# Out projection inside the second attention, and attention layers in a hand-made issue order, on one Trainium2 core

## The chip, the cores and the metric

The kernel runs on one core of one Trainium2 chip (trn2). The metric is device time in microseconds (us) of one execution. Each kernel was timed in turn with the kernel before, on the same chip and in the same rounds. The experiments came in five batches on five chips, so kernels of different batches are compared by their ratios to the kernel before (whose medians lay between 1346.9 and 1352.4 us) and by the stages of their profiles.

Engine names in the profile: PE is TensorE (PEld its weight loads), DVE is VectorE, ACT is ScalarE, POOL is GpSimd, SP is SyncE. A name with q (SPq) is the sequencer of that engine that issues DMA transfers. L408 is line 408 of the kernel that the line belongs to. PSUM is the memory that matmuls write to; an eviction is the op that copies a result out of it.

## The reference

Four layers in the order A B A B, each added to its input, on x of 2048 rows by 576 columns. Cut to what matters:

```python
def _A_ref(x, wqkv, wo):            # sliding-window attention, 32 heads of 18
    qkv = (x @ wqkv)                # -> q, k, v
    # every query looks at 8 keys: its own row and rows 2, 4, ..., 14 before it
    logits = einsum('bhsd,bhswd->bhsw', q, kg) * scale
    o = einsum('bhsw,bhswd->bhsd', softmax(masked logits), vg)
    return o.reshape(B, S, D) @ wo

def _B_ref(x, w_in, w_sp, b_sp, w_out):      # gated MLP with a mix over rows
    z = gelu(x @ w_in)                       # 576 -> 4608
    z1, z2 = halves of z                     # 2304 each
    z2 = layernorm(z2)
    g = w_sp @ z2 + b_sp[:, None]            # 2048 x 2048 over rows
    return (z1 * g) @ w_out                  # 2304 -> 576

x = x + A(layernorm(x)); x = x + B(layernorm(x))
x = x + A(layernorm(x)); x = x + B(layernorm(x))
```

## The kernel before

**Attention.** The rows are cut into 19 query tiles of 112 rows, each with 16 rows of halo, and the 32 heads into two halves. That makes 38 steps. A step computes logits (16 small matmuls, `L_mm`), exponentials on ScalarE (`EXP`), a mask on VectorE (`MASK`), the product with V (`PV`) and the division by the row sum (`NORM`). The result of a tile is transposed by a DMA (`TAIL_A`) and goes through the output projection `wo` and the residual add (`TAIL_B`). Then it is normalised for the next layer and transposed again. The projections to Q, K and V are spread over the steps. The program order below is only a proposal: a scheduler fixes the order on each engine, and it is told to put the next logits ahead.

```python
        def pr(off):
            return tc.high_priority(offset=off) if off > 0 else nullcontext()
        for s in range(NSTEP):                     # cfg.prio = 200, cfg.prio2 = 0
            with pr(cfg.prio2):
                EXP(s)
                MASK(s)
            if s + 1 < NSTEP:
                with pr(cfg.prio):
                    L_mm(s + 1)
            if s >= 1:
                with pr(cfg.prio2):
                    PV(s - 1)
                    NORM(s - 1)
            for fn in table.get(s, []):            # Q/K, V, tail work of this step
                fn()
        # ... [cut] where the tail of tile t goes (plast = its second step):
            for (off, fn) in ((2, TAIL_A(t)), (4, TAIL_B(t)), (5, TAIL_B2(t)), (6, TAIL_C(t))):
        # steps after the Q/K work also get two junk matmuls each (JUNK)
```

Every third eviction of Q/K is on VectorE, the others on ScalarE, and the moves that lay the heads out (`QK<-stg`) go over three engines' queues:

```python
                use_dve = (self.evac_rr % 3 == 0)
                if use_dve:
                    nc.vector.tensor_copy(out=dst, in_=pp[:, :])
                else:
                    nc.scalar.copy(out=dst, in_=pp[:, :])
                # ... [cut] one move of 72 KB per head: sync, gpsimd or scalar queue in turn
```

**B layer.** First the "norm stage": 16 tiles of z2, gelu, statistics and normalisation. Each tile is normalised by nine ops of 256 columns, most of them on VectorE, the rest on GpSimd. Then the "mixer": z1, the 2048 by 2048 mix, bias and product. Then a separate out projection, whose weights are loaded only when the mixer's buffers are free:

```python
        def p1_norm(i):
            for b in range(NB):                    # NB = 9 blocks of 256 columns
                if b >= NB - NPOOL_NORM:
                    nc.gpsimd.tensor_scalar(out=z2b[b][:, i, :], ...)
                else:
                    nc.vector.tensor_scalar(out=z2b[b][:, i, :], ...)
        # ... [cut] mixer
        wout_b = p3.tile([P, NJ - NJA, D], bf16, name="wout_b", bufs=1)
        for j in range(NJA, NJ):
            self.dma(wout_b[:, j - NJA, :], wv_[:, j, :], eng=(nc.sync, nc.gpsimd)[j % 2])
        # ... [cut] then 16 row tiles: p3_mm (36 matmuls), residual add, statistics, normalise, transpose
```

The softmax here doesn't subtract the row's maximum and nothing guards it: scores larger than these inputs give would overflow.

## Time and profile before

The kernel before takes 1347.1 us (median of four runs, 1344.7 to 1348.4). The page of the profile gives TensorE as the busy engine. These are whole lines of its parts 1 (busy time), 2 (busy tenths in 40 slices of the span; PEclk is the granted TensorE clock in tenths of full speed) and 4 (the chain of work that ended last):

```profile
span 1348.4 us, 21451 instructions
...
PE 1249.9 (93%) x8656; PEld 659.5 (49%) x8656; DVE 616.5 (46%) x1402; ACT 384.2 (28%) x595; POOL 356.4 (26%) x487
...
PE   1999969989999999998998987899999999999997
...
PEclk9999989999999999997999999899999999999999
...
PE 62%; DVE 11%; POOL 10%; issue 7%; DMA 6%; ACT 3%; SPq 1%; ACTq 0%; POOLq 0%; DVEq 0%
...
```

TensorE is busy 93% of the time, and the clock is near full almost everywhere. A gain can come only from the 7% of gaps and from matmuls that could be left out. The view of stretches cuts the span at the stages. Its columns are the stretch, its length, busy time and instruction count of each engine (PE, PEld, DVE, ACT, POOL), the granted clock, the DMA share and GB/s:

```profile
...
46.50:188.00 141.50, 125.74 (x1771) 78.17 (x1771) 102.60 (x240) 82.76 (x111) 70.90 (x59) 0.96 0.63 114
...
274.30:605.00 330.70, 326.96 (x1515) 147.58 (x1512) 104.11 (x161) 39.35 (x44) 9.82 (x20) 1.00 0.05 16
605.00:690.00 85.00, 77.18 (x582) 58.56 (x581) 36.06 (x99) 13.01 (x15) 17.05 (x39) 0.92 0.71 200
690.00:849.00 159.00, 141.19 (x1840) 84.94 (x1839) 107.49 (x248) 88.92 (x120) 77.30 (x96) 0.97 0.62 125
...
```

From the top: the steps of the first attention (TensorE busy 126 of 141.5 us), the first mixer (327 of 331, fixed by the matmuls), the first out projection (77 of 85), and the second attention (141 of 159). The last out projection, not shown, takes 84 us, TensorE busy in 73. The view of TensorE's waits from 605 to 849 us (who waited for whom, us in total, times, longest) shows how little is lost:

```profile
...
PE po_6066 L941 <- DMA wout_b<-in_B_w_out_dram: 7.1, 6, 2.1
PE O_ps L540 <- DVE ln_rstd L163: 4.0, 9, 0.7
PE pw L582 <- DMA oT_7004<-o_t_6991: 3.9, 1, 3.9
...
```

The wait for w_out at the start of the projection is the largest.

VectorE closes the loop of the norm stage. This is its timeline (start, duration, operation, and in brackets the idle time before it):

```profile
...
229.40 0.34 DVE L848 TENSOR_SCALAR z2b_3093<-zp,z_mean,z_rstd 128x256 bf16<-128x256 bf16 x1 [0.67 <-POOL z_rstd L835]
...
231.10 1.77 DVE L819 CUSTOM_DVE_ANT_0 z_junkD<-zp 128x1536 bf16<-128x1536 bf16 x1
...
234.41 0.35 DVE L848 TENSOR_SCALAR z2b_3093<-zp,z_mean,z_rstd 128x256 bf16<-128x256 bf16 x1 [0.67 <-POOL z_rstd L835]
...
```

From 229.40 to 234.41 is one period of 5.02 us (start times are rounded). Six such ops of 256 columns, then a sum of squares of 1.77 us and small ops.

### The profile page before, as it was taken

The numbers are of one execution on the slowest core, as the hardware profiler recorded it, in microseconds if no ns is written. First come the engines' busy times: TensorE is split into PE (matmuls) and PEld (weight loads), VectorE is DVE, ScalarE is ACT, GpSimd is POOL, SyncE is SP. The second block draws the span as 40 slices with busy tenths as digits, with TensorE's granted clock in tenths as the row PEclk, the third lists the DMA queues.
The fourth block names the chain that finished last, engine by engine and source line by source line (L and its number), as shares of the span: only waits on it lengthen the run. The fifth ranks groups of instructions, "written<-read, shape, count | busy, mean of one in ns | idle before, by whom it ended". The sixth has DMA issues, their size and how long they took to land.

```text
span 1348.4 us, 21451 instructions
## 1 busy us (share of the span) xinstructions
PE 1249.9 (93%) x8656; PEld 659.5 (49%) x8656; DVE 616.5 (46%) x1402; ACT 384.2 (28%) x595; POOL 356.4 (26%) x487
## 2 busy tenths in 40 slices
PE   1999969989999999998998987899999999999997
PEld 0456644434444444445754655444444444444576
DVE  4468858843322332332534878588323223333221
ACT  2556726620011111001126665465101111100000
POOL 7445547830000000002141646488000000000111
PEclk9999989999999999997999999899999999999999
DMA  9449759020000000009653677861100000000232
GB/s 264 98 94 145 121 134 214 1 90 6 9 10 9 10 9 9 0 4 266 179 137 62 151 145 129 181 125 41 43 9 9 10 9 9 2 7 1 72 113 67
DMA packets 180128, 101.04 MB, mean 75 GB/s; under 512 B 138276, under 2 KB 162212, under 8 KB 180028
## 3 DMA queue, kind: packets, MB, share of 16 engines
q1 hardware_dynamic: 170208, 84.15, 28.1%
q10 hardware_dynamic: 6364, 8.55, 2.2%
q0 software_dynamic: 3456, 6.96, 2.2%
q8 instruction: 68, 1.11, 0.3%
q14 instruction: 32, 0.26, 0.1%
HBM read 41.16 MB, written 16.52 MB: 43 GB/s over the span
## 4 chain that ended last, share of the span: by engine, by line
PE 62%; DVE 11%; POOL 10%; issue 7%; DMA 6%; ACT 3%; SPq 1%; ACTq 0%; POOLq 0%; DVEq 0%
PE pg L904 36%; PE po L941 9%; DVE z_junkD L819 4%; PE pp L412 3%; DMA QK<-stg 2%; POOL ln_xn_84 L181 2%; POOL ln_xn_81 L181 1%; POOL ln_rstd L164 1%; POOL z_rstd L835 1%; POOL ln_xn_83 L181 1%; POOL ln_xn_82 L181 1%; DMA wout_b<-in_B_w_out_dram 1%; DMA wv_sb<-in_A_wqkv_dram 1%; DMA win2b<-in_B_w_in_dram 1%; DVE z_msq L828 1%
## 5 line engine op out<-in xcount | busy, mean ns | idle before, releaser
L908 DVE TENSOR_TENSOR g_tmp<-pg,bsp 128x512 f32<-128x512 f32 x144 | 99.4, 692 | 435.5 <-PE pg L904 423.9
L412 PE MATMUL pp<-xnT,wqk_sb 128*128 128x512 bf16 x400 | 100.7, 394 | 29.8 <-DMA xnT<-ln_xn_84 28.5
L812 PEld LDWEIGHTS <-xnT 128*128 128x128 bf16 x800 | 78.4, 98 | 97.0 <-issue 13.0
L812 PE MATMUL pz<-win2a,xnT 128*128 128x512 bf16 x384 | 103.1, 379 | 5.9 <-ACT zp L816 4.4
L164 POOL TENSOR_TENSOR ln_rstd<-ln_rstd,neg_half 112x1 f32<-112x1 f32 (+2 forms) x70 | 43.4, 621 | 152.3 <-DVE ln_rstd L163 152.1
L812 PE MATMUL pz<-win2b,xnT 128*128 128x512 bf16 x256 | 77.0, 386 | 6.9 <-DMA win2b<-in_B_w_in_dram 6.9
L816 ACT ACTIVATE zp<-pz 128x1024 bf16<-128x1024 f32 x64 | 65.0, 1020 | 44.6 <-POOL z2b_9746 L845 18.9
L412 PEld LDWEIGHTS <-wqk_sb 128*128 128x128 bf16 x400 | 36.9, 100 | 71.2 <-issue 36.0
L819 DVE CUSTOM_DVE_ANT_0 z_junkD<-zp 128x1536 bf16<-128x1536 bf16 x32 | 56.9, 1777 | 18.7 <-ACT zp L816 18.7
L370 PE MATMUL pv<-wv_sb,xnT 128*128 128x288 bf16 (+1 forms) x380 | 62.2, 286 | 0.2 <-DVE stg L418 0.2
L76 POOL DMA_DIRECT2D wout_b<-in_B_w_out_dram x14 | 7.5, 541 | 172.4 <-PE pg L904 172.4
L76 POOL DMA_DIRECT2D QK<-stg x52 | 31.5, 608 | 73.0 <-ACT stg L420 28.0
L584 DVE TENSOR_TENSOR x_new<-pw,xo 112x288 f32<-112x288 f32 (+1 forms) x76 | 33.5, 445 | 18.0 <-PE pw L582 10.7
L420 ACT CAST stg<-pp 128x512 bf16<-128x512 f32 x54 | 31.0, 585 | 37.4 <-PE pp L412 22.7
L370 PEld LDWEIGHTS <-xnT 128*128 128x128 bf16 (+1 forms) x380 | 33.5, 97 | 15.8 <-issue 1.4
L489 PE MATMUL L_ps<-QK 18*128 18x112 bf16 (+1 forms) x1216 | 32.0, 210 | 4.9 <-DMA QK<-stg 1.7
L418 DVE CAST stg<-pp 128x512 bf16<-128x512 f32 x26 | 18.0, 691 | 37.0 <-PE pp L412 33.5
L159 DVE BATCH_NORM_STATS2 ln_st<-x_new 112x6 f32<-112x288 f32 (+1 forms) x76 | 33.9, 449 | 1.2
L489 PEld LDWEIGHTS <-QK 18*128 18x128 bf16 (+1 forms) x1216 | 20.4, 93 | 25.6 <-issue 21.6
L845 POOL TENSOR_SCALAR z2b_3101<-zp,z_rstd,z_nmr 128x256 bf16<-128x256 bf16 x16 | 32.4, 2024 | 0.0
L845 POOL TENSOR_SCALAR z2b_9746<-zp,z_rstd,z_nmr 128x256 bf16<-128x256 bf16 x16 | 32.4, 2023 | 0.0
L904 PE MATMUL pg<-W_sb,z2b_3093 128*128 128x512 bf16 x128 | 28.4, 379 | 1.9 <-DVE z2b_3093 L848 1.9
(549 smaller groups left out, 2513.3 us busy)
## 6 DMA issues: line engine op xcount, KB each, us to landing
xres_73<-x_new SPq DMA_DIRECT2D x18, 252.0 KB
xo<-xres_74 SPq DMA_DIRECT2D x18, 252.0 KB
xres_75<-x_new SPq DMA_DIRECT2D x18, 252.0 KB
QK<-stg POOLq DMA_DIRECT2D x52, 72.0 KB, 3.8
win2a<-in_B_w_in_dram SPq DMA_DIRECT2D x2, 1728.0 KB
QK<-stg SPq DMA_DIRECT2D x48, 72.0 KB
wqk_sb<-in_A_wqkv_dram ACTq DMA_DIRECT2D x4, 576.0 KB
out_dram<-ob SPq DMA_DIRECT2D x16, 144.0 KB
```

What stands on the lines that cost most here:

```text
L164: nc.gpsimd.tensor_tensor(out=rstd[:nrows, :], in0=rstd[:nrows, :], in1=self.neg_half[:nrows, :], op=ALU.pow)
L181: e.tensor_scalar(out=xn[:nrows, 0:D], in0=x_t[:nrows, :], scalar1=mv[:nrows, 0:1], scalar2=rstd[:nrows, 0:1], op0=ALU.subtract, op1=ALU.mult)
L370: nc.tensor.matmul(pv[:nk, 0:288], lhsT=self.xnT[:, c, QT * t:QT * t + nk], rhs=wv_sb[:, c, hh * 288:(hh + 1) * 288], start=(c == 0), stop ...
L412: nc.tensor.matmul(pp[:, :], lhsT=wqk_sb[:, c, wc0:wc0 + P], rhs=self.xnT[:, c, col0:col0 + 512], start=(c == 0), stop=(c == 4))
L489: nc.tensor.matmul(L_ps[:nk, j, ftl * QT:ftl * QT + nq], lhsT=kT[32 * j:32 * j + DH, g, QT * t:QT * t + nk], rhs=qT[32 * j:32 * j + DH, g, ...
L812: nc.tensor.matmul(pzvs[ci][:, sub * 512:sub * 512 + w], lhsT=self.xnT[:, c, PADL + i * P:PADL + (i + 1) * P], rhs=win2(c)[:, c0 + sub * 5 ...
L816: nc.scalar.activation(out=zp[:, c0:c0 + cn], in_=pzvs[ci][:, 0:cn], func=ACT.Gelu_apprx_tanh, accum_out=sums[:, ci:ci + 1])
L819: nc.vector.tensor_tensor_reduce(out=junkD[:], in0=zp[:, 0:SQ_D], in1=zp[:, 0:SQ_D], scale=1.0, scalar=0.0, op0=ALU.mult, op1=ALU.add, acc ...
L845: nc.gpsimd.tensor_scalar(out=z2b[b][:, i, :], in0=zp[:, b * 256:(b + 1) * 256], scalar1=rstd[:, 0:1], scalar2=nmr[:, 0:1], op0=ALU.mult, ...
L904: nc.tensor.matmul(pg[:, :], lhsT=z2b[jj][:, i, sub * P:(sub + 1) * P], rhs=W_sb[:, i, q * 512:(q + 1) * 512], start=(i == 0), stop=(i == ...
L908: nc.vector.tensor_tensor(out=tmp[:], in0=pg[:, :], in1=bsp[:, q * 512:(q + 1) * 512], op=ALU.add)
L941: nc.tensor.matmul(acc[hh], lhsT=uT[j // 2][:, j % 2, i * P:(i + 1) * P], rhs=wout_j(j)[:, hh * 288:(hh + 1) * 288], start=(j == 0), stop= ...
```

## The change

The intent is to fill the gaps of one stage with the work of another. The out projection of the first B layer is to run inside the second attention, whose steps leave TensorE idle. Therefore its weights are loaded during the mixer, and the mixer's results stay in place in one set of buffers (`zc`). The Q/K projections go in five chunks of rows, so that attention can start before all rows are known. In the attention layers the order on every engine is written by hand (`manual_schedule`), with no scheduler, no priorities and no junk matmuls. The core of the diff, with cuts:

```diff
-        for s in range(NSTEP):
-            with pr(cfg.prio2):
-                EXP(s)
-                MASK(s)
-            if s + 1 < NSTEP:
-                with pr(cfg.prio):
-                    L_mm(s + 1)
-            # ... [cut]
+        self.run_deferred()
+        with tc.manual_schedule():
+            run(pro)
+            L_mm(0)
+            for s in range(NSTEP):
+                EXP(s)
+                if s >= 1:
+                    PV(s - 1)
+                    NORM(s - 1)
+                run(tabA.pop(s, []))        # out projection of a tile, V, transposes of o
+                MASK(s)
+                if s + 1 < NSTEP:
+                    L_mm(s + 1)
+                run(tabB.pop(s, []))        # Q/K projections, units of w_out, statistics
+                run(tabE.pop(s, []))        # normalise + transpose, late loads
+        # the tail of tile t:
+        tl = 3 if first else 2
+        for t in range(NT):
+            p_ = 2 * t + 1
+            put(tabA, p_ + 1, t_load, t)
+            put(tabA, p_ + 1, t_oT, t)              # issue the transpose of o
+            put(tabA, p_ + tl, t_half, t, 0)        # use it
+            put(tabA, p_ + tl + 1, t_half, t, 1)
+            put(tabB, p_ + tl + 1, t_stats, t)
+            put(tabE, p_ + tl + 2, t_ln, t)
+        # Q/K: evictions all on ScalarE, one run of columns per head, q and k together
+                nc.scalar.copy(out=stg[:, qk * w:(qk + 1) * w], in_=pp[:, 0:w])
+                        self.dma(QK[c][32 * rg:32 * rg + DH, g, :], stg[...],
+                                 eng=(nc.gpsimd if j7 % 2 else nc.sync))
+        # the fused out projection: a half unit, 18 matmuls into one PSUM buffer
+        def u_half(i, hh):
+            po = self.PT_tile("po")
+            self.p3_mm(i, hh, po)
+            nc.vector.tensor_tensor(out=x3[...], in0=po[:, 0:288], in1=xo3[...], op=ALU.add)
         # B layer
         def p1_norm(i):
-            for b in range(NB):   # nine ops of 256 columns on VectorE and GpSimd
-                # ... [cut]
+            nc.vector.tensor_scalar(out=zc[i // 4][:, i % 4, 256:256 + Fh], in0=zp[:], ...)  # 2304 columns
+        # w_out: two loads of 1.3 MB on GpSimd's queue, written at jj == 2 of the mixer
+            self.dma(self.wout[:, 0:h, :], src[:, 0:h, :], eng=self.nc.gpsimd)
+        # second half of w_in (2.3 MB): one load on the sync queue at step 14 of the first attention
+            self.dma(win2[:, 0:4, :], self.B_w_in[0:512, Fh:2 * Fh].rearrange("(c p) n -> p c n", p=P))
```

Outside the attention layers the scheduler still decides.

## The prediction

> **What bounds the kernel now.** By the table of stretches: first attention 0 to 188 us; its B layer's norm stage to 274, mixer to 605, out projection to 690; second attention to 849; norm to 935, mixer to 1264.5, out projection to 1348. In the mixers TensorE is 100% busy: the chain of waits shows blocks of 18.13 us for 84 matmuls of 512 columns, 0.216 us each. About 660 us are so fixed. Gaps are elsewhere: attention steps after the Q/K work take 2.85 us with PE busy 61 of 72 us and DVE 60, partly junk matmuls (88, 27 us summed); steps with Q/K take about 5.3 us. The norm stage repeats every 5.02 us, against 4.86 us of matmul issue: by the timeline VectorE closes that loop (six normalise ops 1.70, square-sum 1.70, small ops 0.93, a 0.67 us wait on GpSimd). It opens with a 3.9 us wait for a weight load. Both out projections open with waits for w_out (12 us stretches, PE busy 5.3 and 9.1 us).
>
> **What the change does, by stage.**
> - Mixer: same matmuls, in the same order; results go in place into shifted columns. About 0.
> - Norm: one VectorE op of 2304 columns replaces six of 256 and three on GpSimd. The six follow each other at 0.26 us, too short for one column per cycle plus overhead. The Trainium skill, "VectorE: DVE Perf Modes", section "Side-by-side: where the cycles go for N=2048 bf16", gives about 0.69 us for 2048 columns in the fastest mode; estimate 0.8 us here. The loop falls to about 4.1, so TensorE binds at 4.86; weights are loaded early. 86.3 becomes about 79: -7, twice.
> - Last out projection: weights preloaded. 576 matmuls at 0.1225 us = 70.6 plus a 7 us end, against 84: -6.
> - First out projection plus second attention: now 244 us. Matmul issue in the fused stage, by traced rates: projection 70.6, Q/K 44, V 23.5, out 23.5, logits 12, PV 16 = 190 us, junk gone. Prologue 45, 38 steps averaging 4.0 us of PE work with 5 to 10% of stalls, tail 7: about 226. -18.
> - First attention: nothing fused to fill with. In the new order VectorE's mask of a step precedes PV, then V and out matmuls, then the residual add, then the next mask: 1.1 + 0.5 + 0.6 + 0.7 + 0.55, about 3.5 us a step, slightly more with Q/K. 38 steps make about 137, starting at about 43 instead of 46.5: 185 against 188. -3.
>
> Summed: -41 to -46 us.
>
> **Predicted: 1304 us**, 8 in 10 between 1278 and 1328. Faster by over 2%: 0.82; within 2%: 0.15; slower: 0.03.
>
> **What would show it.** Right: norm period about 4.9 us, the 2304-column op under 1 us; mixer end to second norm stage 215 to 237 us, PE busy above 85%; first attention 175 to 192; no wait for w_out at the end; mixer blocks still 18.1 us. Wrong: the wide normalise near 2.4 us; PE waiting on masks or transposes in fused steps, or on Q/K moves at a chunk's first logits (160 moves a layer instead of 64, 70 on GpSimd at 0.6 us of issue each).
>
> **What would make it wrong.** Fixed order: a late transpose, move or eviction blocks the matmuls behind it, and nothing overtakes. Three shared PSUM buffers serve all projections; all Q/K and V evictions are on ScalarE. The first attention could lose 10 us so. With near perfect overlap the fused stage nears 205 us, and the total 1280.

## The result, and the profile after

The kernel after is correct and takes 1434.6 us (median of four runs, 1430.3 to 1436.6). The ratio is 1.0648, 95% interval 1.0617 to 1.0678: slower. Ratios here are the mean time of one kernel's fast runs over that of the other's in the same rounds, so they are not quite the ratio of the medians quoted.

The same parts of the page:

```profile
span 1434.9 us, 21392 instructions
...
PE 1261.4 (88%) x8592; PEld 676.7 (47%) x8668; DVE 575.8 (40%) x1200; ACT 420.1 (29%) x696; POOL 244.7 (17%) x371
...
PE   5677869989999999998766776689899999999999
...
PEclk9797969999999999999888998679999999999999
...
PE 76%; DMA 9%; ACT 4%; DVE 4%; issue 2%; SPq 1%; POOL 1%; ACTq 0%; DVEq 0%; POOLq 0%
...
```

TensorE has nearly the same number of matmuls as before: 8668 weight loads instead of 8656, that is 100 more Q/K matmuls (narrower ones) and no junk ones (88). (Of the matmuls themselves only 8592 were recorded.) Yet it is busy 11 us longer, and its clock has dips to 0.6, 0.7 and 0.8 in the two attention stages, where before has one 7 and two 8s. In the row PE the dips stand at the same places. The view of stretches of the kernel after, from the top: the steps of the first attention, the first mixer, and the fused stage in three parts, namely the prologue (the work before the first logits), the steps from the first logits to the last, and the tail:

```profile
...
39.70:217.30 177.60, 129.97 (x1748) 82.29 (x1748) 110.31 (x257) 97.62 (x155) 93.04 (x109) 0.82 0.50 118
...
296.60:631.70 335.10, 327.70 (x1483) 148.34 (x1512) 101.64 (x151) 38.95 (x42) 4.29 (x6) 0.99 0.06 18
631.70:675.60 43.90, 38.54 (x280) 27.11 (x278) 12.37 (x35) 12.86 (x22) 13.12 (x38) 1.00 0.60 175
675.60:933.10 257.50, 181.89 (x2091) 121.11 (x2092) 116.03 (x272) 100.97 (x157) 88.70 (x111) 0.86 0.43 109
933.10:945.90 12.80, 6.74 (x69) 3.83 (x66) 6.44 (x20) 1.51 (x3) 3.67 (x4) 0.50 0.43 104
...
```

The steps of the first attention take 177.6 us (before: 141.5). The fused stage takes 43.9 + 257.5 + 12.8 = 314.2 us, of which TensorE is busy 38.5 + 181.9 + 6.7 = 227.2. Its prologue takes what was predicted (45); the loss is in the steps. Before, projection and attention together took 85 + 159 = 244. The norm stage and the last projection became shorter (table below), and the mixer became longer.

This table takes the stages from the first and last matmuls of the traces, in us. Later columns belong to experiments told below:

| stage | before | predicted | after | x_comb3 | x_auto3 | h1 |
|---|---|---|---|---|---|---|
| first attention with its start | 188.1 | 185 | 217.3 | 193.8 | 195.2 | 198.2 |
| norm stage, first | 86.3 | 79 | 79.3 | 82.2 | 79.2 | 81.9 |
| mixer, first | 330.5 | 330.5 | 335.1 | 328.4 | 327.8 | 328.4 |
| out projection + second attention | 243.7 | 226 | 314.2 | 252.6 | 244.7 | 233.3 |
| norm stage, second | 86.9 | 80 | 78.5 | 79.6 | 78.9 | 82.5 |
| mixer, second | 328.8 | 328.8 | 335.2 | 328.5 | 329.9 | 327.6 |
| last out projection | 84.1 | 78 | 75.3 | 75.2 | 75.2 | 75.2 |
| profiled span | 1348.4 | | 1434.9 | 1340.3 | 1330.9 | 1327.1 |

Against the prediction the fused stage lost 88 us, the first attention 32 and the two mixers 11 together; the rest was right or slightly better.

**What TensorE waits for.** In the fused stage:

```profile
...
PE pw L408 <- DMA oT_5984<-o_t_5981: 21.4, 5, 8.0
PE pw L408 <- DMA oT_5983<-o_t_5980: 18.8, 6, 7.9
PE pw L408 <- DMA oT_5985<-o_t_5982: 14.3, 5, 5.0
PE L_ps L351 <- ACT P_sb_5978 L359: 8.9, 10, 1.9
...
```

The first three lines are one tile with three buffers: 54.5 us in 16 waits for a transposed attention output, up to 8.0 us each. In the first attention it is the same wait, and as large a one for the exponentials that free the logits' PSUM:

```profile
...
PE pw L408 <- DMA oT_113<-o_t_110: 11.2, 3, 6.6
PE L_ps L351 <- ACT P_sb_107 L359: 10.6, 9, 3.8
PE L_ps L351 <- ACT P_sb_108 L359: 10.2, 11, 1.8
...
```

**The longest of these waits, step by step.** TensorE's timeline, at 125 us:

```profile
...
122.13 0.78 PE L329 MATMUL pv<-wv_sb,xnT 128*128 128x288 bf16 x5
...
125.62 0.55 PE L377 MATMUL O_ps<-v_ext_103,P_sb_108 128*128 128x19 bf16 x16
132.78 1.38 PE L408 MATMUL pw<-wo_sb,oT_113 128*128 128x288 bf16 x5 [6.61 <-DMA oT_113<-o_t_110]
133.96 1.40 PE L329 MATMUL pv<-wv_sb,xnT 128*128 128x288 bf16 x5
135.29 0.58 PE L351 MATMUL L_ps<-zc_70 18*128 18x112 bf16 x16
...
```

The five `pw` matmuls wait 6.61 us. Everything that follows in the order waits with them: V, and the logits of the next step; neither shows a wait of its own when its turn comes. Then the clock is low. Five `pv` matmuls take 1.40 us instead of 0.78, and 16 logits 0.58 instead of 0.40. This is what the Trainium skill describes in "TensorE: Matmul & The Clock Gate", section "Part 1: The HAM clock gate (the "warmup" mystery)": an idle window of about 3.4 us lets the clock fall to half, and about 3.4 us of work bring it back. The trace agrees for this wait (1.40 / 0.78 = 1.8; the view of stretches gives a granted clock of 0.50 from 128.3 to 138.5 us). But a wait need not be that long: the clock also went to 0.50 at 107.8, 152.2 and 199.9 us, where no wait just before was longer than 2.2 us and TensorE had been busy for 1.9, 1.7 and 2.2 of the 3.4 us before. Nor does every wait have this effect: of the 16 in the fused stage, 11 were followed by half clock. So a wait is often paid twice. In the two attention stages together TensorE was busy 379.0 us here and 358.0 in x_comb3 (below) for the same matmuls, at a higher clock there and still not a full one. The sync queue in the same microseconds:

```profile
...
117.79 1.20 SPq L64 DMA_DIRECT2D win_119<-in_B_w_in_dram  x2
...
120.64 3.05 SPq L64 DMA_DIRECT2D zc_68<-stg  x4
123.73 0.46 SPq L64 DMA_DIRECT2D xo<-in_A_x_dram  x1
129.54 1.24 SPq L401 DMA_TRANSPOSE oT_113<-o_t_110  x1
...
```

A load of w_in (2.3 MB) is issued at 117.79. Behind it stand a store, four Q/K moves and a small load, and only then, at 129.54, the transpose that TensorE waits for; it takes over 3 us to land. The queue itself stood still for 5.3 us before it, and the profile puts that down to the landing of the load:

```profile
...
SPq L401 <- DMA win_119<-in_B_w_in_dram: 5.3, 1, 5.3
...
```

**Why a step with Q/K work takes 4.5 to 5.5 us.** ScalarE's timeline in the first attention:

```profile
...
92.70 1.71 ACT L359 ACTIVATE P_sb_108<-L_ps 128x896 bf16<-128x896 f32 x2
94.30 0.41 ACT L333 CAST v_ext_102<-pv 128x288 bf16<-128x288 f32 x1
95.99 0.55 ACT L311 CAST stg<-pp 128x464 bf16<-128x464 f32 x1 [1.28 <-PE pp L309]
96.97 0.55 ACT L311 CAST stg<-pp 128x464 bf16<-128x464 f32 x1 [0.43 <-PE pp L309]
97.42 0.87 ACT L145 ACTIVATE ln_xn_73<-x_in_334,ln_nmr,ln_rstd 128x576 bf16<-128x576 bf16 x1
98.19 1.71 ACT L359 ACTIVATE P_sb_107<-L_ps 128x896 bf16<-128x896 f32 x2
...
```

and TensorE's logits in that time:

```profile
...
94.47 0.40 PE L351 MATMUL L_ps<-zc_69 18*128 18x112 bf16 x16 [1.38 <-ACT P_sb_108 L359]
94.81 2.13 PE L309 MATMUL pp<-xnT,wqk_sb 128*128 128x464 bf16 x10
...
```

The logits of the next step are done at 94.87. Their exponentials start at 98.19, 3.3 us later: in ScalarE's order stand a V eviction, two Q/K evictions and a normalise op, and the evictions wait for ten `pp` matmuls. The Trainium skill, "Perfetto Trace Analysis", section "Tensor Engine Instruction (MATMUL, LD_WEIGHTS)", says that ScalarE, VectorE and GpSimd are strict first-in-first-out; this timeline agrees. Late steps without Q/K work do run at about 3.4 us: exponentials start at 170.92, 174.69, 177.93 and 181.12 us.

**The mixer's extra 5 us** is one wait, at its first matmul:

```profile
...
PE pz_4025 L679 <- DMA w_0_4019<-in_B_w_in_dram: 5.8, 1, 5.8
```

This line is from the kernel after. In GpSimd's timeline the two halves of w_out (1.3 MB each) are issued at 297.07 and 300.64 us, ahead of the mixer's own first weights (301.73 on the sync queue), and the bias follows. The scheduler had moved the load there from its place in the text, two blocks later. In the second mixer the same.

### The profile page after: what moved, and what is told of

Read it like the earlier page. It is cut to its first block, busy times and chain, and to the rows that moved or that the text cites. A ratio compares the mean times of both kernels' runs of the same rounds, so it can differ in the third digit from the quotient of the medians.

```text
span 1434.9 us, 21392 instructions
## 1 busy us (share of the span) xinstructions
PE 1261.4 (88%) x8592; PEld 676.7 (47%) x8668; DVE 575.8 (40%) x1200; ACT 420.1 (29%) x696; POOL 244.7 (17%) x371
## 4 chain that ended last, share of the span: by engine, by line
PE 76%; DMA 9%; ACT 4%; DVE 4%; issue 2%; SPq 1%; POOL 1%; ACTq 0%; DVEq 0%; POOLq 0%
PE pg L690 34%; PE pz L616 10%; PE po L212 9%; PE pp L309 5%; PE pw L408 3%; PE pv L329 2%; DMA oT_5983<-o_t_5980 1%; PE L_ps L351 1%; PE pzs L616 1%; ACT P_sb_108 L359 1%; DMA oT_5984<-o_t_5981 1%; DMA oT_5985<-o_t_5982 1%; DMA win_119<-in_B_w_in_dram 1%; PE O_ps L377 1%; ACT stg L311 1%
## 5 line engine op out<-in xcount | busy, mean ns | idle before, releaser
L690 PE MATMUL pg<-W_sb,zc_68 128*128 128x512 bf16 x570 | 148.1, 381 | 0.1
L690 PE MATMUL pg<-W_sb,zc_70 128*128 128x512 bf16 x560 | 146.3, 379 | 1.3
L690 PE MATMUL pg<-W_sb,zc_69 128*128 128x512 bf16 x560 | 146.3, 380 | 0.6
L690 PE MATMUL pg<-W_sb,zc_71 128*128 128x512 bf16 x564 | 146.2, 379 | 0.6
L132 POOL TENSOR_TENSOR ln_rstd<-ln_rstd,neg_half 112x1 f32<-112x1 f32 (+2 forms) x70 | 39.0, 558 | 523.0 <-DMA wo_sb<-in_A_wo_dram 340.6
L309 PE MATMUL pp<-xnT,wqk_sb 128*128 128x464 bf16 (+1 forms) x500 | 112.4, 381 | 11.7 <-DMA xnT<-ln_xn_73 4.1
L616 PEld LDWEIGHTS <-xnT 128*128 128x128 bf16 x800 | 78.9, 99 | 80.9 <-issue 4.8
L690 PEld LDWEIGHTS <-zc_68 128*128 128x128 bf16 x576 | 56.6, 98 | 68.2 <-issue 1.1
L690 PEld LDWEIGHTS <-zc_71 128*128 128x128 bf16 x576 | 56.4, 98 | 68.5 <-DVE zc_71 L643 0.8
L690 PEld LDWEIGHTS <-zc_69 128*128 128x128 bf16 x576 | 56.5, 98 | 68.3 <-issue 0.6
L690 PEld LDWEIGHTS <-zc_70 128*128 128x128 bf16 x576 | 56.4, 98 | 67.7
L329 PE MATMUL pv<-wv_sb,xnT 128*128 128x288 bf16 (+1 forms) x380 | 69.4, 325 | 17.5 <-POOL mask_base L97 13.5
L311 ACT CAST stg<-pp 128x464 bf16<-128x464 f32 (+1 forms) x100 | 50.8, 514 | 101.5 <-PE pp L309 82.9
L309 PEld LDWEIGHTS <-wqk_sb 128*128 128x128 bf16 x500 | 49.7, 106 | 60.8 <-issue 22.5
L619 ACT ACTIVATE zp<-pz 128x1024 bf16<-128x1024 f32 x64 | 65.5, 1024 | 38.7 <-PE pz L616 38.5
L616 PE MATMUL pz<-win_119,xnT 128*128 128x512 bf16 x312 | 72.6, 384 | 1.1 <-DVE x_new L410 0.5
L616 PE MATMUL pz<-win_8983,xnT 128*128 128x512 bf16 x312 | 71.9, 381 | 1.1 <-DVE x_new L410 0.5
L329 PEld LDWEIGHTS <-xnT 128*128 128x128 bf16 (+1 forms) x380 | 41.1, 110 | 33.6 <-POOL mask_base L97 13.5
L386 DVE RECIPROCAL rec<-O_ps 112x16 f32<-112x16 f32 (+1 forms) x76 | 19.2, 253 | 71.9 <-PE O_ps L377 71.7
## 6 DMA issues: line engine op xcount, KB each, us to landing
zc_68<-stg SPq DMA_DIRECT2D x72, 32.6 KB
```

The source lines that it names most:

```text
L132: nc.gpsimd.tensor_tensor(out=rstd[:nrows, :], in0=rstd[:nrows, :], in1=self.neg_half[:nrows, :], op=ALU.pow)
L309: nc.tensor.matmul(pp[:, 0:w], lhsT=Aw["wqk"][:, k_, wc0:wc0 + P], rhs=self.xnT[:, k_, lo:lo + w], start=(k_ == 0), stop=(k_ == 4))
L311: nc.scalar.copy(out=stg[:, qk * w:(qk + 1) * w], in_=pp[:, 0:w])
L329: nc.tensor.matmul(pv[:nk, 0:288], lhsT=self.xnT[:, c, QT * t:QT * t + nk], rhs=Aw["wv"][:, c, hh * 288:(hh + 1) * 288], start=(c == 0), s ...
L616: nc.tensor.matmul(pz[:, k_ * 512:k_ * 512 + w], lhsT=lhs[c], rhs=win2[:, c, c0:c0 + w], start=(c == 0), stop=(c == 4))
L619: nc.scalar.activation(out=zp[:, us[0][0]:us[0][0] + w], in_=pz[:, 0:w], func=ACT.Gelu_apprx_tanh, accum_out=sums[:, ns:ns + 1])
```

## The experiments

The theory to begin with was that the order written by hand is at fault, since a late input blocks everything behind it on its engine (called the order below). Rivals:

- the lead: transposes are issued one step (second attention) or two (first) ahead of their use, too few;
- ScalarE's order: evictions stand ahead of exponentials;
- the fusion: the projection's matmuls delay the attention chain;
- the queue: the sync queue is too full of Q/K moves for transposes to be issued in time. Where an expectation names a theory Q, it is this one.

Eighteen kernels ran on the chip. Unless told otherwise each was timed twice, and h1 and the three of the last batch four times. All gave correct results.

### x_auto: the scheduler's order back

```diff
-        with tc.manual_schedule():
+        if True:
```

> The changed kernel with only the fixed issue order lifted: the scheduler orders all engines again, all else as in the change. Theory A (the fixed order costs the time; fusion and one-run moves are harmless): both attention stages shrink, the first from 217 to about 190 us, the fused one from 313 to about 250, total 1330 to 1350. Rival F (fusing the projection and moving Q/K in 160 moves a layer cost the time themselves): stays above 1410.

1388.4 us (ratio 1.0291, interval 1.017 to 1.041, wide because each side has only two runs: one of the three of the kernel before was an outlier of 4472 us and was left out). Theory A had expected 1330 to 1350. The order is worth 46 us of the loss. But 41 us of loss stay, the first attention still takes 213.6 us, and the fused stage 267.7. The order is a cause and not the only one.

### x_tl4, x_actlate, x_unfused: one rival each, in the fixed order

x_tl4 gives the transposes three steps of lead, the use coming four steps after the tile's last step (and it moved the load of the residual with the use):

```diff
-        tl = 3 if first else 2
+        tl = 4
-            put(tabA, p_ + 1, t_load, t)
+            put(tabA, p_ + tl - 1, t_load, t)
```

> Fixed order kept; the output matmuls of a tile come 4 steps after its last PV instead of 3 and 2 (the residual load moves with them). Theory T (matmuls are stuck behind transposes that the DMA queue delivers late: 54.5 us of such waits in the fused stage and 16 in the first attention[...]): these waits nearly vanish and the total falls by 60 to 90 us, to 1345 to 1375. Rival S (ScalarE's order, evictions and normalise ops standing between one exp and the next, sets the step): the waits move to the exp loop and the gain is 30 us or less.

1434.1 us, where theory T had expected 1345 to 1375. The fused stage fell to 287.0 us, but the first attention rose to 238.7. VectorE now waited for the residual there:

```profile
...
DVE x_new L410 <- DMA xo<-in_A_x_dram: 42.9, 12, 9.4
...
```

That was a flaw of the edit: the residual's load now stood late in the sync queue. It is mended in x_tl4b below.

x_actlate holds the Q/K evictions and the normalise ops of a step back behind the next exponentials on ScalarE (with the transposes and late loads that stand with the normalise ops in `tabE`):

```diff
             for s in range(NSTEP):
                 EXP(s)
+                run([(fn, ()) for fn in late])      # evictions of the step before
+                late.clear()
+                run(tabE.pop(s - 1, []))            # normalise ops of the step before
```

> Fixed order kept; on ScalarE the Q/K evictions and the normalise ops of a step come after the next step's exp instead of before it. Rival S: steps of the first attention with Q/K fall from 5.5 us to about 4.4, so that stage goes from 217 to about 195 us, and the fused one loses 10 to 25 us: total about 1390. Theory T: less than 15 us in all, since the transposes stay late.

1436.2 us: nothing. The waits tell why. In the first attention:

```profile
...
PE pw L422 <- DMA oT<-o_t: 31.1, 10, 8.8
...
PE L_ps L365 <- ACT P_sb L373: 5.2, 2, 5.1
...
```

The wait of the logits for the exponentials fell from 20.8 us (10.6 + 10.2 above) to 5.2, as meant. The wait for the transposes rose from 16.3 us (11.2 + 3.4 + 1.7) to 31.1. One limit went, and the next took all its time.

x_unfused does all 16 units of the out projection ahead of the second attention, in the same fixed order:

```diff
-            for i in range(4):
-                P_(u_load, i + 1)
+            for i in range(NS):
+                if i + 1 < NS:
+                    P_(u_load, i + 1)
                 P_(u_half, i, 0)
             # ... [cut]
-            units([(i, hh) for i in range(8, 12) for hh in range(2)], 6, 10)   # and the three like it
```

> Fixed order kept; all 16 tiles of the first out projection run before the second attention, so the fusion alone is undone. If fusing is worth what was meant, this is slower than the change. If it hurts in this order (the projection's matmuls and its normalise ops lengthen every step and delay the transposes), mixer end to second norm stage goes from 313 us to about 82 + 178 = 260 us and the total to about 1380.

1436.7 us, with 317.5 us for projection and attention, against 314.2 fused. The fusion falls as a cause: it neither cost nor gained anything in this state.

### x_pool, x_tl4b, x_comb, x_autopool: the queue, and repairs together

x_pool puts all Q/K moves on GpSimd's queue, so that the sync queue has only transposes, loads and stores:

```diff
-                                 eng=(nc.gpsimd if j7 % 2 else nc.sync))
+                                 eng=nc.gpsimd)
```

> Fixed order kept; all Q/K moves are issued by GpSimd, none by the sync queue, whose issues fill 136 of 177 us of the first attention's steps (73 moves, 59 us) in one first-in first-out line with the transposes. Theory Q (the transposes that the output matmuls wait for are late because they stand behind moves in that line): the transposes come in time, first attention from 217 to 190-200 us, fused stage from 314 to 265-285, total about 1375. If the line is not the cause: within 15 us of the change, or slower because GpSimd, at 0.55 us a move and 2.3 us a normalise op, becomes the late one.

1457.2 us (ratio 1.0806): worse by 23 us. The remedy of the queue theory fails. That doesn't yet say that the full queue costs nothing, since GpSimd now has a cost of its own.

x_tl4b is x_tl4 with the residual's load left early and one or two more buffers for it:

```diff
-        tl = 3 if first else 2
+        tl = 4
-            xo = sb.tile([P, D], x_dt, name="xo", tag="xo", bufs=2)
+            xo = sb.tile([P, D], x_dt, name="xo", tag="xo", bufs=4)
-            ... name="x_new", tag="x_new", bufs=3)
+            ... name="x_new", tag="x_new", bufs=4)
```

> The 4-step distance again, without the fault of the first trial, in which the residual load moved with the matmuls and VectorE waited 39 us for it in the first attention: here the load stays early and has two more buffers. Theory T (distance from transpose to matmul): first attention 195 to 205 us, fused stage 265 to 285, total 1370 to 1385. If instead ScalarE's order or the queue's throughput sets the step: first attention stays at 213 to 217 and the fused stage gains 27 us or less.

1401.1 us (ratio 1.039). The fused stage fell from 314.2 to 275.5 us, and the transpose waits in it from 54.5 us to 4.4:

```profile
...
PE L_ps L351 <- ACT P_sb L359: 16.2, 20, 2.0
...
PE pw L408 <- DMA oT<-o_t: 4.4, 2, 2.7
...
```

The first attention did not gain (217.3 us, 195 to 205 expected). So the lead (with the buffers that it needs) was the largest of the single causes tried within the fixed order, by way of the fused stage alone. Now the exponentials (first line, 16.2 us) come first, so that ScalarE's order should count.

x_comb puts the three together (`pool`, `tl4b`, `actlate`), and x_autopool is x_auto with x_pool's edit.

> All three at once in fixed order: moves on GpSimd, 4-step distance with buffers, evictions and normalise ops after the next exp. If the three are stacked limits, each hiding the next, this gains more than their sum: first attention about 175 to 185 us, fused stage 235 to 255, total 1325 to 1345. If something else limits (step chain through VectorE, GpSimd): above 1370.

> Scheduler's order and moves on GpSimd. The scheduler's order alone left transpose waits of 29.6 and 25.8 us in the two attention stages. Theory Q: these shrink to under 10 us each and the total falls from 1388 to about 1355. If not the line: stays near 1385.

x_comb took 1389.4 us, where 1325 to 1345 would have meant that the three limits are all; above 1370 something else limits. x_autopool took 1381.6: against x_auto its interval (1.0216 to 1.0276) lies inside the other's, and its transpose waits are 24.5 and 19.6 us where theory Q wanted under 10. So in the scheduler's order the place of the moves made no clear difference. In x_comb the sync queue itself waited in the first attention:

```profile
...
SPq L153 <- POOL ln_rstd L132: 69.4, 11, 12.9
...
```

L153 is the transpose of the normalised rows. It was issued 69.4 us late in sum, behind GpSimd, which raises to the power and normalises, and now also issues all moves. The transposes of o stand behind it in the same queue. So a new rival came up: normalising on GpSimd delays the queue.

### x_lnact, x_tl4late, x_comb2, x_comb3: the repairs one upon the other

x_lnact normalises on ScalarE alone; x_tl4late is `tl4b` + `actlate`, without `pool`; x_comb2 is x_tl4late + x_lnact; x_comb3 adds the loads: w_out on the sync queue, meant to stand behind the mixer's first weights, and w_in in five pieces spread over the steps.

```diff
-            tstate[t] = (x_new,) + self.ln_stats(sb, x_new, nq, t >= NT - 2)
+            tstate[t] = (x_new,) + self.ln_stats(sb, x_new, nq, True)         # x_lnact, x_comb2, x_comb3
-            self.dma(self.wout[:, 0:h, :], src[:, 0:h, :], eng=self.nc.gpsimd)
+            self.dma(self.wout[:, 0:h, :], src[:, 0:h, :])                    # x_comb3, both halves
-            put(tabE, 14, win2_load)
+            for c in range(5):
+                put(tabE, 12 + 4 * c, win2_load, c)                           # x_comb3; steps 26 + 2 * c in the second
```

> The changed kernel with one thing altered: the attention tiles' normalise op runs on ScalarE (0.87 us there) instead of GpSimd (2.3 us). Theory G (GpSimd's slow normalise op holds the sync queue, where the transpose that waits for it stands ahead of the next tile's output transpose; 69 us of such waits in the last combined trial): both attention stages gain, 10 us or more each. Rival: the op now stands in ScalarE's line ahead of the next exp, waiting for GpSimd's small ops, and nothing or less than nothing is won in this order.

> 4-step distance with buffers, and evictions and normalise ops after the next exp; moves shared by the sync queue and GpSimd as in the change. Against the combined trial it undoes only the moves' transfer to GpSimd. Theory G: GpSimd is relieved of 90 moves a layer, so it is faster than the combined trial: first attention about 200 us against 213, fused stage about 258 against 269. Theory Q (the sync queue): slower than the combined trial.

> The previous one plus the normalise op on ScalarE, after the next exp. Theory G: first attention 175 to 188 us, fused stage 235 to 250; total near 1335. If neither falls by 8 us against the previous one, GpSimd's normalise op is not the limit.

> The previous one plus the big weight load in five pieces over 16 or 8 steps instead of one 2.3 MB load in the middle of an attention, and w_out loaded by the sync queue behind the mixer's first weights. Each stretch with the load lost some 8 us (one wait of 6.6 us for a transpose behind it, then half clock): two times 5 to 10 us. The mixers lost 5 and 7 us to a wait for their first weights behind w_out: back to 329 to 331 us each. Total 20 to 30 us under the previous one.

| kernel | edits | us | ratio to before | first attention | second with projection | mixer |
|---|---|---|---|---|---|---|
| after | | 1434.6 | 1.0648 | 217.3 | 314.2 | 335.1 |
| x_actlate | ScalarE's order | 1436.2 | 1.0645 | 213.2 | 317.2 | |
| x_lnact | normalise on ScalarE | 1417.9 | 1.0525 | 217.8 | 295.5 | |
| x_tl4b | lead | 1401.1 | 1.039 | 217.3 | 275.5 | 335.3 |
| x_tl4late | lead + ScalarE's order | 1370.1 | 1.017 | 203.5 | 260.2 | 334.6 |
| x_comb2 | + normalise on ScalarE | 1361.0 | 1.0103 | 198.7 | 254.6 | |
| x_comb3 | + loads | 1341.7 | 0.9959 | 193.8 | 252.6 | 328.4 |

ScalarE's order is worth nothing alone and 31 us once the lead is there. Normalising on ScalarE is worth 17 us alone, all of it in the fused stage, and 9 us behind the other two. That is less than theory G said: in x_comb2 the two stages fell by 4.8 and 5.6 us, under the 8 us that the expectation had set, so by this test GpSimd's normalise op was no longer the limit there. The gains don't add, as with limits that lie one behind the other. The edit of the loads is worth 19 us, of which about 6 in each mixer (334.6 against 328.4) and 5 in the first attention. The wait at the mixer's start is nearly gone, 0.8 us instead of 5.8, though only half of the plan came about: in x_comb3's timeline of the sync queue the first half of w_out is still issued ahead (276.21 us), then the mixer's weights (281.05), then the second half (283.25). With x_comb (1389.4) against x_tl4late (1370.1), which differ only in the place of the moves, the remedy of the queue theory fails once more in the fixed order: taking the moves back from GpSimd is worth 19 us (18 by the ratios, since the two ran in different batches). What a full sync queue costs by itself stays open, since no run emptied it without loading another engine. x_comb3 is level with the kernel before: 0.9959, interval 0.993 to 0.9988.

### x_auto3, x_comb3u, h1: order, fusion and the old attention

x_auto3 has x_comb3's repairs with the scheduler's order (and without `actlate`, which only a fixed order needs). x_comb3u is x_comb3 with the fusion undone as in x_unfused. h1 takes the attention of the kernel before, with its scheduler order, priorities, junk matmuls and moves, and the B layer of the kernel after with the loads of x_comb3: one wide normalise op, w_out loaded during the mixer, w_in in pieces. Its out projection is separate, as before.

```diff
 # h1, against the kernel after: layer_A is that of before (cut), and
+    def mid_out(self, li):                       # the first out projection, separate
+        for i in range(cfg.NS):
+            for hh in range(2):
+                po = self.PT_tile("po")
+                self.p3_mm(i, hh, po)
+                # ... [cut] residual add, store, statistics, normalise, transpose
-            self.dma(self.wout[:, 0:h, :], src[:, 0:h, :], eng=self.nc.gpsimd)
+            self.dma(self.wout[:, 0:h, :], src[:, 0:h, :])
```

> The repaired kernel without its fixed order (distance, normalise op on ScalarE, weight load in pieces, w_out late, all kept; the scheduler orders the engines). If the fixed order is still a cost: faster than 1342 us by 10 or more. If, once repaired, it is as good as the scheduler's: within 10 us or slower.

> The repaired kernel with the fusion alone undone. If fusing now pays, mixer end to second norm stage is longer than 253 us: 72 us of projection plus some 155 to 160 of steps plus latencies gives 235 to 245 if steps are like the first attention's, so I expect it 5 to 15 us faster unfused, meaning that fusing costs more in steps than it fills. Fusion pays if it comes out above 258.

> The old attention (scheduler's order, chunks of 1024, moves in two runs, projection apart) with the change's B layer: one wide normalise op, all weights of the norm stage and w_out loaded early, w_out behind the mixer's first weights. If the B layer's parts are gains in their own right: norm stages 79 us each, mixers 329 each, last projection 74, first projection about 75 instead of 85; attention 188 and about 160 as before; total about 1308 to 1318.

- x_auto3: 1328.3 us (1324.0 to 1332.6), ratio 0.9858, interval 0.9817 to 0.9898. After the repairs the scheduler is worth 13 us (1341.7 against 1328.3), where ahead of them it was worth 46.
- x_comb3u: 1345.3 us, ratio 0.9984. The stage takes 258.0 us against 252.6 fused. So the fusion is worth about 5 us of its stage in these two profiles, once the order works; the intervals of the two kernels' ratios overlap (0.993 to 0.9988, 0.996 to 1.0008), so that a gain in the whole time is not shown. 18 were predicted.
- h1: 1325.9 us (1322.6 to 1329.0), ratio 0.9832, interval 0.981 to 0.9853. It is the fastest in the medians, with the *old* attention; x_auto3 is not separable from it. Both beat the two kernels, by less than 2% but clear of the noise; 1308 to 1318 were expected of h1. Its gain is in the stages that the prediction had right (see the table above): 4.4 us in each norm stage, 9 at the end, and 10 in projection plus attention, where the waits for w_out (7.1 us before) are gone. Its first attention is 10 us slower than before. Of this 2 us lie before the first logits, and waits for output transposes are 7.9 us instead of 4.0; why they are longer stays open.

### x_auto3d, x_auto3p, x_auto3pd: what is left in the attention

In x_auto3 the first attention still takes 195 us against 188 before. Two differences were left to try: evictions (every third Q/K eviction on VectorE, d) and the priority of the next logits (p); pd has both.

```diff
-                nc.scalar.copy(out=stg[...], in_=pp[:, 0:w])
+                rr[0] += 1
+                if rr[0] % 3 == 0:
+                    nc.vector.tensor_copy(out=stg[...], in_=pp[:, 0:w])       # d
+                else:
+                    nc.scalar.copy(out=stg[...], in_=pp[:, 0:w])
-                    L_mm(s + 1)
+                    with tc.high_priority(offset=200):
+                        L_mm(s + 1)                                           # p
```

> The repaired kernel in the scheduler's order (1328 us), with every third Q/K eviction on VectorE as in the kernel before. Theory (a), ScalarE's queue is what is left: the waits of TensorE on ScalarE evictions shrink, first attention falls from 195 to 190 us or less, fused stage from 245 to 238 or less, total 1312 to 1320. If ScalarE is not what is left: within 4 us of 1328.

> The repaired kernel in the scheduler's order (1328 us), with the next step's logits at the high priority that the kernel before gave them. Theory (b), the priority is what is left: first attention falls to 190 us or less and the total to 1312 to 1320. If not: within 4 us of 1328, or slower, since other matmuls are then pushed back behind the logits.

> Both edits. If (a) and (b) are independent causes the gains add: 1298 to 1312. If only one of them is a cause, this run equals the better of the two single edits within 4 us.

1333.3, 1328.8 and 1331.6 us, against 1328.3 of x_auto3 in another batch; ratios 0.9891, 0.9865 and 0.9878 against 0.9858. None gains. (The profiled first attentions, 198.1, 192.0 and 196.0 us, lean to the priority, but the timed runs show no gain.) Neither is the cause of the 7 us that are left, which stays open. The traces say where to look: waits for output transposes come first again in this stage, 14.4 us in x_auto3 and 14.2 in x_comb3 against 4.0 before.

## Why the prediction was right or wrong

**Right: the norm stage.** Predicted -7 twice, measured -7.0 and -8.4 us. The wide op takes 0.88 us as recorded (0.8 estimated from the Trainium skill, "VectorE: DVE Perf Modes", section "Side-by-side: where the cycles go for N=2048 bf16"):

```profile
...
L643 DVE TENSOR_SCALAR zc_68<-zp,z_mean,z_rstd x8: 878/879/881, 228.0 to 970.1; 128x2304 bf16<-128x2304 bf16 x8
...
```

The numbers are the shortest, median and longest duration in ns, and the first and last start. A tile repeats every 4.84 us (the op on tile 12 starts at 286.1, 58.1 us after the one on tile 0).

**Right: the last projection.** Predicted -6, measured -9. No wait for w_out appears in it.

**Right in mechanism: the mixer's blocks**, but the stage was called "About 0" and lost 4.6 and 6.4 us. The early load of w_out was counted as a gain only. It went ahead of the mixer's own first weights. x_comb3, with only the second half of w_out behind them, has 328.4 and 328.5 us.

**Wrong: "38 steps averaging 4.0 us of PE work with 5 to 10% of stalls ... about 226".** This is the step of the prediction that failed most, 88 of the 131 us by which the total missed. The prologue was right (43.9 us for 45). The steps took 257.5 us from the first logits to the last, 7.0 us each: 4.9 of TensorE's work instead of 4.0, the low clock included (4.5 in x_comb3), and 2.0 of stalls, 29%, where 0.2 to 0.4 were allowed. 54.5 us of the stage were waits for transposes issued one step before their use. In the fixed order each also held the independent matmuls behind it, and most put the clock down. The prediction named this ("a late transpose, move or eviction blocks the matmuls behind it, and nothing overtakes") among what could make it wrong, and gave it a cost of 10 us in the first attention, and a chance of 3% to a slower kernel at all. What it did not do is compare the lead of each transfer, in steps, with the time from its issue's turn in the queue to its landing. x_tl4b shows that more lead alone takes 39 us off the stage.

**Wrong: "about 3.5 us a step, slightly more with Q/K. 38 steps make about 137".** Steps without Q/K do take about 3.4 us. Steps with Q/K take 4.5 to 5.5, because the sum followed VectorE and TensorE, and left out the order on ScalarE (exponentials behind evictions behind matmuls). With the start taken off the steps took 177.6 us. That ScalarE's order is a limit is shown by x_tl4late against x_tl4b: 203.5 against 217.3 us. It shows only once the lead is repaired.

**Wrong in size: the worth of the fusion, "-18".** x_comb3 against x_comb3u puts it at 5 us of the stage when the order is repaired (not separable in the whole time), and x_unfused at about none in the change as given. In the fused stages TensorE is still the engine with the work, yet not full: busy 213.6 of 252.6 us in x_comb3, where the largest wait is now that of the Q/K matmuls for the normalised and transposed rows (12.7 us).

**Not what the signals said.** Of the three signals for "wrong" (a normalise op near 2.4 us; waits on masks or transposes; waits on Q/K moves at a chunk's first logits), only the transposes came true. Waits on masks were 6.8 us in the fused stage. No wait on a Q/K move is among the larger ones, although there are 160 moves a layer.

**What stays open.** The first attention in the new form is 4 to 10 us slower than before even after all repairs (192.0 to 198.1 in the last six kernels), and the old attention in h1 is too (198.2). Evictions and priority are not the reason. The gains of single repairs depend on the order in which they are made, so no fixed share of the 87 us belongs to one of them; what is shown is that four repairs in the fixed order give back 93 us, and that the scheduler alone gives back 46.

## What to carry to other kernels

When the order is written by hand, list for every transfer the steps between its issue and its use, and for every engine what stands ahead of the op on the longest chain; a sum of busy times only says what the stage can't be faster than. Expect several limits of nearly the same length: if removing one changes nothing, look in the waits for the one that took its time, and repair them together before judging any. A preload costs what it delays: look at which loads it goes ahead of. Here it was enough to have half of it behind the ones that are needed first.

## What the Trainium skill lacked or had wrong

- "DMA: Bandwidth & Descriptors", section "Issuing engines are not separate DMA queues", says that issuing on several engines saves only the sequencer's time, "which is usually small relative to the DMA itself". In the first attention of the kernel after it is not small: the sync queue spent some 130 us of 177.6 on issuing (136 by the merged rows of its timeline; Q/K moves of up to 32.6 KB about 0.7 us each, transposes about 1.2 us), and where the trace gives it, for those on GpSimd's queue, such moves land 2 to 3 us after their issue. Where to issue mattered in the fixed order: putting the moves all on GpSimd cost 23 us (x_pool), and taking them off it again gave 19 (x_comb to x_tl4late). In the scheduler's order it made no clear difference (x_auto to x_autopool).
- "VectorE: DVE Perf Modes", the section cited above: its sum of columns / 4, 8 and about 150 cycles at 0.96 GHz gives 764 ns for 2304 columns, an estimate; recorded were 879 ns. Recorded durations of ops of 256 columns (340 ns) also exceed their spacing (260 ns), so that some 80 ns of it may overlap the next op.
- No page has the case that the runs show most clearly: limits that lie one behind the other in first-in-first-out queues, so that single repairs measure as nothing (x_actlate +1.6 us alone, -31 us behind x_tl4b).
